# One TensorE task for both token halves of a head pair's sums, with both small PSUM banks

## The chip, the cores and the metric

One core of a Trainium2 chip runs the whole program. The metric is device microseconds for one execution. Three runs of the kernel before took 1083.85, 1081.62 and 1084.06 us, median 1083.85. The execution that was profiled took 1081.87 us by its own time, and its profile spans 1080.1 us.

## What is computed

Attention with a memory term, then two feed-forward layers, all float32:

```python
scores = scale * np.matmul(q, k.transpose(0, 1, 3, 2))     # B=4, H=8, S=576, D=64
scores = np.where(causal, -1000000000.0, scores)
a = softmax(scores)                                        # rows, + 1e-09
local = np.matmul(a, v)
mem_out = einsum(phi(q), M_prev) / (einsum(phi(q), z_prev) + 1e-06)
x = g * mem_out + (1 - g) * local                          # g = sigmoid(beta), to [2304, 512]
h = x @ w_in;  x = (h * tanh(log1p(exp(h)))) @ w_out       # d_ff = 2048
h = x @ w2_in; out = (h * cos(h)) @ w2_out
```

## The kernel before, in words

**Tasks and their order.** Every step of the work is a task with an engine, a cost, the tasks that it needs, a rank, the buffers that it takes and those that it uses (`add`, L163). `arrange` (L176) runs a model of the engines by these costs and lays the tasks out in one list; each engine then executes its own in that order, and the semaphores that the framework sets keep the data right. An engine waits at the instruction it has come to and passes none. Where TensorE (PE) would have nothing to do early in the program, `arrange` puts short dummy matmuls in (`warm`, L303).

**Attention.** Sixteen pairs of heads are done one after the other, overlapping (`pair`, L346; the pair's number stands in the tiles' names, so `pv9_0` is pair 9's). PE transposes k and q (`ptk`, `ptq`, L400), evacuated by ScalarE (ACT) or VectorE (DVE) to `kT` and `qT`, and at the last keys also to `kd`. Scores are made in three groups of rows (`s`, L491), and one small piece of 64 keys goes into a bank of its own (`sx`, L511); DVE takes the row maxima (L520, L524), ACT the exponentials (L536), DVE sums and scales (L563, L572). PE transposes the scaled rows (`t`, L587), ACT or DVE copies them to `PT`. Then the sums of heads: `pv`, L654, tokens 0 to 287 in one task (`pv..._0`, 6 matmuls), 288 to 575 in another (`pv..._1`, 10 matmuls), each evacuated to `xs` (`f_xs`) and stored to DRAM (`f_out`, L663).

**Banks.** `ptk`, `ptq`, `sx`, `t` and `pv` share two PSUM banks, the pool `misc`. A task that takes one holds it until all users of its tile are through: for `sx` that is two maxima on DVE and two exponentials on ACT. Before, each half of the sums takes one bank; `pv(1)` also names `pv(0)`'s matmuls and copy among what comes before it. `arrange` asks for each buffer that a task takes when it will be free. For the small banks it looks at the one whose turn is next; the turn moves only when the task is laid out:

```python
            o = held[b.cls][turn[b.cls] % len(held[b.cls])]      # L206, in at_free(b)
...
                    for b in t.takes:                            # L233
                        f = at_free(b)
...
                for b in t.takes:                                # L275
                    held[b.cls][turn[b.cls] % len(held[b.cls])] = b
                    turn[b.cls] += 1
```

**The rest.** From some 106 us on PE fills the time between attention's steps with the first layer's first half of d_ff, in blocks of 256 tokens (`h0`, L759, `acc0`, L802; block 0 needs the stored halves 0 of pairs 0 to 3, L699 loads it). At about 375 us attention is over. Its memory is then given to the first layer's second half and the second layer, in blocks of 384 tokens (L887, L967, L969), to the end.

Of the kernel before, what the change touches and what calls it, by code (L numbers as in the profile page):

```python
# [29 lines left out]
def tile_kernel(ctx: ExitStack, tc: tile.TileContext, q, k, v, M_prev, z_prev, beta,  # L30
                moe_w_in, moe_w_out, moe2_w_in, moe2_w_out, out):
    nc = tc.nc
    B, H, S, D = q.shape
# [129 lines left out]
    def add(eng, cost, fn, deps=(), rank=0.0, takes=(), uses=(), func=None, mode=0, lag=0.0, size=0):  # L163
        t = Task()
        t.eng, t.cost, t.fn, t.rank, t.takes = eng.split("/"), cost, fn, rank, list(takes)
        t.func, t.mode, t.lag, t.end, t.on, t.size = func, mode, lag, None, None, size
        t.deps = [d for d in deps if d is not None]
        for b in (*takes, *uses):
            b.users.append(t)
        tasks.append(t)  # L170
        return t
# [141 lines left out]
    def copy(e, dst, src, scale=None):  # L313
        if e == "act":
            nc.scalar.activation(dst, src, AF.Copy, scale=1.0 if scale is None else scale)  # L315
        elif scale is None:
            nc.vector.tensor_copy(out=dst, in_=src)  # L317
        else:
            nc.vector.tensor_scalar(out=dst, in0=src, scalar1=scale, scalar2=None, op0=ALU.mult)

    def c_act(n):
        return 0.19 + 0.00082 * n

    def c_dve(n):
        return 0.11 + 0.00106 * n

    def c_both(n):
        return (c_act(n), c_dve(n))
# [5 lines left out]
    ROWS = [D] + [P] * 4  # L334
    START = [0] + [D + P * i for i in range(4)]
    SLOTS = ((3, 0), (4,), (2, 1))
    PARTS = ((0, SH), (SH, S))
# [3 lines left out]
    def misc(name):  # L341
        return pools["misc"].tile([P, 512], F32, tag="m", name=name)
# [3 lines left out]
    def pair(m):  # L346
        b, h0 = m // NP, 2 * (m % NP)
        hp = m % NP
        d = {}
        A1, A2 = pools["a1"], pools["a2"]  # L350
        R = 100.0 * m
        B_ = {n: Buf(n) for n in ("q", "k", "v", "z", "mv", "mn", "ph", "qT", "kT", "kd", "PT", "xs")}
# [29 lines left out]
        dv = add("sp", 1.8, f_v, rank=R + 5, takes=[B_["v"], B_["mv"]], size=320)  # L382
# [206 lines left out]
        flipped = {}  # L589
# [32 lines left out]
        for x, order_ in enumerate(SLOTS):  # L622
            for i in order_:
# [6 lines left out]
                else:  # L630
                    flip(i, [(i, 0, j) for j in range(na)],
                         lambda PT, i=i, na=na: PT[:, i + 1:i + 2 + 6 * (na - 1):6, :], x)
                    flip(i, [(i, 1, i - y) for y in range(na)],
                         lambda PT, i=i, na=na: PT[:, 24 - 6 * i:24 - 6 * i + 7 * (na - 1) + 1:7, :], x)
                    if i == 4:
                        flip(4, [(4, 1, 0), (4, 0, 4)], lambda PT: PT[:, 28:30, :], x)

        def pv(x):
            lo, hi = PARTS[x]
            w = hi - lo  # L640
            bm = Buf("misc")
            s = {}
            js = [j for j in range(5) if START[j] < hi]

            def f_pv(e):
                PT, vt = d["PT"].rearrange("p b c -> p (b c)"), d["v"]
                s["o"] = o = misc(f"pv{m}_{x}")
                for j in js:
                    z_ = max(START[j], lo)
                    first_a, first_b = (7 * j + 1) * P - START[j], (24 - 6 * j) * P - START[j]  # L650
                    if j == 0:
                        first_a, first_b = first_a + D, first_b + D
                    for h, c in ((0, first_a), (1, first_b)):
                        nc.tensor.matmul(o[h * D:(h + 1) * D, z_ - lo:w], vt[:, h, j - 1, :] if j else d["mv"][:, h, :],  # L654
                                         PT[:, c + z_:c + hi], start=j == 0, stop=j == js[-1])

            def f_xs(e):
                if x == 0:
                    d["xs"] = A2.tile([P, S], F32, tag="xs", name=f"xs{m}")
                copy(e, d["xs"][:, lo:hi], s["o"][:, 0:w])  # L660

            def f_out(e):
                nc.sync.dma_start(out=x1d[b][:, hp, lo:hi], in_=d["xs"][:, lo:hi])  # L663

            need = [t_ for i in range(5) if START[i] < hi and START[i] + ROWS[i] > lo for t_ in flipped[i]]
            cost = sum(hi - max(START[j], lo) for j in js) * 4 / 2400 + 0.1
            t_p = add("pe", cost, f_pv, need + [dv, p_0], R + 60, [bm], [B_["PT"], B_["v"], B_["mv"]], mode=2)
            t_x = add("act/dve", c_both(w), f_xs, [t_p, x_0], R + 60, [B_["xs"]] if x == 0 else [], [bm] + ([B_["xs"]] if x else []))
            x1_done[m, x] = add("sp", 0.4, f_out, [t_x], -1.0, [], [B_["xs"]], size=144)
            return t_p, t_x  # L670

        p_0 = x_0 = None
        p_0, x_0 = pv(0)
        pv(1)

# [380 lines left out]
    for m in range(NJ):  # L1058
        pair(m)
# [32 lines left out]
    for i in range(4 * NFH, 8 * NFH):  # L1092
        x = i - 4 * NFH
# [36 lines left out]
```

## Time and profile before

| | |
|---|---|
| median of three runs | 1083.85 us |
| the profiled execution | 1081.87 us, span 1080.1 us |
| PE busy | 1053.2 us, 98% of the span |
| DVE, ACT busy | 761.6 us, 570.1 us |
| attention with its overlap | 0 to about 375 us |

The profile has a row for every instruction. PE's matmuls are pipelined, so the time from one row's start to the next row's start is what a group costs. Idle time before an instruction is named after the semaphore that ended it. A line of a wait names a helper (L315, L317: copies by ACT and DVE), so the tile's name says what was waited for.

### The profile page before, as it was taken

To read this page: it belongs to the slowest core of one execution; us is meant where nothing else is said; L and a number is where in the kernel's file an instruction comes from. 1 tells how busy PE (TensorE), PEld (TensorE's weight loads), DVE (VectorE), ACT (ScalarE), POOL (GpSimd) and SP (SyncE) were. 2 spreads that over 40 slices of the span, in tenths; PEclk is the share of its full clock that TensorE was granted. 3 is DMA by queue.
4 is the path that set the end of the run, shared out by engine and by line. 5 is a ranking of instruction groups with operands and counts; after the bars stand their busy time and mean duration, and the time that the engine had idled before them with its cause. 6 is when DMAs were issued, how large, how long until landed. Compare 5 with 4: busy or idle time off the path is not lost.

```text
span 1080.1 us, 17930 instructions
## 1 busy us (share of the span) xinstructions
PE 1053.2 (98%) x6938; PEld 938.7 (87%) x6938; DVE 761.6 (71%) x1694; ACT 570.1 (53%) x1279; POOL 3.8 (0%) x19
## 2 busy tenths in 40 slices
PE   8898999999999999999999999999999999999998
PEld 5666778788877899989999999998999999999997
DVE  6999997886787568757552228887666676766664
ACT  4676675676676443433323234766555555555544
POOL 1000000000000000000000000000000000000000
PEclk9999999999999999999999999999999999999999
DMA  6455423222322165446352216211000010000000
GB/s 165 114 132 161 113 55 103 69 70 67 100 69 59 44 204 156 137 135 205 102 183 88 89 59 187 79 38 59 1 30 30 1 59 2 30 30 1 30 1 30
DMA packets 112853, 88.73 MB, mean 82 GB/s; under 512 B 65792, under 2 KB 103680, under 8 KB 112768
## 3 DMA queue, kind: packets, MB, share of 16 engines
q1 hardware_dynamic: 112768, 87.58, 27.1%
q8 instruction: 55, 0.90, 0.3%
q14 instruction: 30, 0.25, 0.1%
HBM read 68.69 MB, written 18.87 MB: 81 GB/s over the span
## 4 chain that ended last, share of the span: by engine, by line
PE 88%; DVE 7%; ACT 3%; issue 1%; POOL 0%; ACTq 0%; POOLq 0%; DVEq 0%
PE h L887 28%; PE acc L969 18%; PE acc L967 9%; PE h L759 9%; PE acc L802 9%; PE pv L654 5%; PE t L587 4%; PE s L491 3%; DVE nm L520 2%; DVE p L572 1%; PE warm L303 1%; ACT p L536 1%; PE ptq L400 1%; ACT PT L315 1%; PE ptk L400 1%
## 5 line engine op out<-in xcount | busy, mean ns | idle before, releaser
L887 PE MATMUL h<-x,w 128*128 128x384 f32 x1728 | 345.0, 337 | 1.6 <-ACT g L903 1.6
L887 PEld LDWEIGHTS h<-x,w 128*128 128x128 f32 x1728 | 307.4, 188 | 17.2 <-ACT g L903 1.8
L969 PE MATMUL acc<-w,G 128*128 128x512 f32 x864 | 228.4, 393 | 0.0
L969 PEld LDWEIGHTS acc<-w,G 128*128 128x128 f32 x864 | 160.0, 188 | 22.1
L954 DVE TENSOR_TENSOR G<-g,G 128x384 fp32r<-128x384 f32 x144 | 79.8, 555 | 100.2 <-ACT G L315 99.6
L759 PE MATMUL h<-x,w 128*128 128x256 f32 x864 | 127.7, 288 | 4.6 <-DVE g L317 4.2
L802 PE MATMUL acc<-G,w 128*128 128x256 f32 x864 | 129.7, 289 | 1.1 <-ACT o L315 0.7
L759 PEld LDWEIGHTS h<-x,w 128*128 128x128 f32 x864 | 111.4, 191 | 9.0 <-DVE g L317 5.2
L315 ACT ACTIVATE G<-g 128x384 fp32r<-128x384 f32 (+1 forms) x152 | 81.2, 535 | 66.6 <-DVE g L938 35.8
L802 PEld LDWEIGHTS acc<-G,w 128*128 128x128 f32 x864 | 111.9, 191 | 4.0 <-ACT o L315 1.4
L967 PE MATMUL acc<-G,w 128*128 128x384 f32 x576 | 112.6, 336 | 0.0
L536 ACT ACTIVATE p<-s,nm 128x64 f32<-128x64 f32 (+4 forms) x160 | 81.3, 515 | 40.0 <-DVE nm L520 26.2
L967 PEld LDWEIGHTS acc<-G,w 128*128 128x128 f32 x576 | 100.9, 188 | 0.0
L931 ACT ACTIVATE n<-n 128x384 f32<-128x384 f32 x96 | 49.9, 521 | 63.5 <-DVE n L927 63.5
L903 ACT ACTIVATE g<-h 128x384 f32<-128x384 f32 x48 | 23.4, 491 | 113.1 <-PE h L887 112.2
L587 PE MATMUL t<-ident,p 128*128 128x128 f32 (+1 forms) x480 | 73.7, 277 | 7.8 <-ACT PT L315 3.7
L520 DVE TENSOR_REDUCE nm<-s 128x2 f32<-128x1024 f32 (+4 forms) x80 | 62.2, 790 | 23.5 <-PE s L495 16.4
L915 DVE TENSOR_SCALAR u<-hs 128x384 f32<-128x384 f32 x96 | 34.5, 359 | 54.6 <-ACT hs L315 51.9
L938 DVE TENSOR_TENSOR g<-n,hs 128x384 f32<-128x384 f32 x96 | 53.2, 555 | 26.3 <-ACT n L934 26.2
L587 PEld LDWEIGHTS t<-ident,p 128*128 128x128 f32 (+1 forms) x480 | 52.3, 140 | 18.5 <-ACT PT L315 7.8
L315 ACT ACTIVATE hs<-h 128x384 f32<-128x384 f32 x96 | 47.0, 490 | 39.3 <-PE h L887 36.6
L315 ACT ACTIVATE PT<-t 128x256 f32<-128x256 f32 (+3 forms) x97 | 43.4, 466 | 42.0 <-PE t L587 41.5
(91 smaller groups left out, 1243.6 us busy)
## 6 DMA issues: line engine op xcount, KB each, us to landing
raw<-in_moe_w_in_dram SPq DMA_DIRECT2D x32, 512.0 KB, 4.3
raw<-in_moe_w_out_dram SPq DMA_DIRECT2D x32, 512.0 KB, 3.8
k<-in_k_dram SPq DMA_DIRECT2D x32, 144.0 KB, 2.8
x1d<-xs SPq DMA_DIRECT2D x32, 144.0 KB, 2.1
xad<-o SPq DMA_DIRECT2D x9, 512.0 KB, 3.7
x2d<-o SPq DMA_DIRECT2D x6, 768.0 KB, 3.6
x<-x2d SPq DMA_DIRECT2D x6, 768.0 KB, 4.2
out_dram<-o SPq DMA_DIRECT2D x18, 256.0 KB, 2.0
```

Source lines behind the costliest of these rows:

```text
L315: nc.scalar.activation(dst, src, AF.Copy, scale=1.0 if scale is None else scale)
L520: nc.vector.tensor_reduce(out=s["nm"][:, c], in_=s["sp"][i], axis=AX.X, op=ALU.max, negate=True)
L536: nc.scalar.activation(d["p", i][:, j, D + lo:D + hi], src, AF.Exp, bias=s["nm"][:, c, j:j + 1], scale=1.0, accum_out=s["sm"][:, 1 if part ...
L587: nc.tensor.transpose(ps[:, at:at + r], d["p", i][0:r, h, j * P:(j + 1) * P], ident[0:r, 0:r])
L654: nc.tensor.matmul(o[h * D:(h + 1) * D, z_ - lo:w], vt[:, h, j - 1, :] if j else d["mv"][:, h, :], PT[:, c + z_:c + hi], start=j == 0, sto ...
L759: nc.tensor.matmul(h[:, half // 2], w[:, a, 0, c * P:(c + 1) * P], x[:, e_, c, :], start=c == 0 and pi == 0, stop=c == NKC - 1 and pi == 2)
L802: nc.tensor.matmul(t[:, c], w[:, a, 1, n * P:(n + 1) * P], G[:, e_, half], start=f == 0 and pi == 0 and c == 0, stop=f == NFH - 1 and pi == 2,
L887: nc.tensor.matmul(q_["h"], w[:, a, 0, c * P:(c + 1) * P], x[:, e_, c, :], start=c == 0 and pi == 0, stop=c == NKC - 1 and pi == 2)
L938: nc.vector.tensor_tensor(out=q_["g"], in0=q_["n"], in1=q_["hs"], op=ALU.mult)
L954: ENG[e].tensor_tensor(out=q_["G"][:, 1], in0=q_["g"], in1=q_["G"][:, 0].bitcast(F32), op=ALU.subtract)
L967: nc.tensor.matmul(o, w[:, a, 1, c * P:(c + 1) * P], G[:, e_, :], start=st, stop=sp_)
L969: nc.tensor.matmul(o, G[:, a, c * P:(c + 1) * P], w[:, e_, 1, :], start=st, stop=sp_)
```

## The change

The two tasks `pv(0)` and `pv(1)` become one, `f_pv`. It needs all of the pair's flipped rows, takes two buffers of the class `misc`, and issues the 6 matmuls of half 0 and then the 10 of half 1. Copies and stores stay one per half, in `out_`; both copies now need the whole task.

```diff
-        def pv(x):
-            lo, hi = PARTS[x]
-            w = hi - lo
-            bm = Buf("misc")
...
+        banks = [Buf("misc") for _ in PARTS]
+        o_ = {}
+
+        def f_pv(e):
+            PT, vt = d["PT"].rearrange("p b c -> p (b c)"), d["v"]
+            for x, (lo, hi) in enumerate(PARTS):
+                o_[x] = o = misc(f"pv{m}_{x}")
+                js = [j for j in range(5) if START[j] < hi]
                 for j in js:
...
+        cost = sum(hi - max(START[j], lo) for lo, hi in PARTS for j in range(5) if START[j] < hi) * 4 / 2400 + 0.1
+        t_p = add("pe", cost, f_pv, [t_ for l in flipped.values() for t_ in l] + [dv], R + 60, banks, [B_["PT"], B_["v"], B_["mv"]], mode=2)
+
+        def out_(x, t_x):
...
-            need = [t_ for i in range(5) if START[i] < hi and START[i] + ROWS[i] > lo for t_ in flipped[i]]
-            t_p = add("pe", cost, f_pv, need + [dv, p_0], R + 60, [bm], [B_["PT"], B_["v"], B_["mv"]], mode=2)
-            t_x = add("act/dve", c_both(w), f_xs, [t_p, x_0], R + 60, [B_["xs"]] if x == 0 else [], [bm] + ([B_["xs"]] if x else []))
+            t_x = add("act/dve", c_both(hi - lo), f_xs, [t_p, t_x], R + 60, [B_["xs"]] if x == 0 else [], [banks[x]] + ([B_["xs"]] if x else []))
             x1_done[m, x] = add("sp", 0.4, f_out, [t_x], -1.0, [], [B_["xs"]], size=144)
...
+        out_(1, out_(0, None))
```

The rest of attention is laid out anew around it, so nearly every pair's order differs. The number of warm matmuls goes from 218 to 216. All other instructions stay in number; a few copies change between DVE and ACT.

**Banks in the program as built.** In 13 of the 16 pairs the two halves lie in different banks. In pairs 1, 9 and 12 `sx` is the task that took a small bank last, its readers come later in the program, and both halves lie in one bank: there the first matmul of `pv..._1` waits for the copy of `pv..._0`. In the other pairs it waits for the copy out of whatever held the second bank. In pairs 5, 8, 13 and 15 that is one of the pair's own flipped rows, in pairs 2, 3, 4, 6, 7 and 10 a `ptk`, in pairs 0, 11 and 14 a `ptq`.

**PE at pair 9's sums**, before (`acc0` and `h0` are the first layer's; the rows left out are `s10_2` and more of these):

```order
L512 MATMUL sx10_3187<-mask2_122,ident_b_120 128x128
L802 MATMUL acc0_1_1_3007<-G0_1_3_2818,w0_6_1853 128x256 x6
L759 MATMUL h0_2_2_3016<-x2_2598,w0_5_1578 128x256 x6
L654 MATMUL pv9_0_3207<-PT9_2993,mv9_2564 64x288 x2
L654 MATMUL pv9_0_3207<-PT9_2993,v9_2561 64x224 x2
L654 MATMUL pv9_0_3207<-PT9_2993,v9_2561 64x96 x2
L802 MATMUL acc0_1_1_3007<-G0_1_3_2818,w0_7_2005 128x256 x6
L491 MATMUL s10_2_3232<-kT10_2821,qT10_2898 128x320 x2
...
L802 MATMUL acc0_2_0_3251<-G0_2_0_3106,w0_1_693 128x256 x6
L654 MATMUL pv9_1_3284<-PT9_2993,mv9_2564 64x288 x2
```

and with the change, where rows that wait for a semaphore name it:

```order
L512 MATMUL sx10_3180<-mask2_122,ident_b_120 128x128
L652 MATMUL pv9_0_3185<-PT9_2999,mv9_2535 64x288 [waits Activation_49]
L652 MATMUL pv9_0_3185<-PT9_2999,mv9_2535 64x288
L652 MATMUL pv9_0_3185<-PT9_2999,v9_2532 64x224 x2
L652 MATMUL pv9_0_3185<-PT9_2999,v9_2532 64x96 x2
L652 MATMUL pv9_1_3192<-PT9_2999,mv9_2535 64x288 [waits Activation_49]
L652 MATMUL pv9_1_3192<-PT9_2999,mv9_2535 64x288
L652 MATMUL pv9_1_3192<-PT9_2999,v9_2532 64x288 x4
```

Half 1 stood 25 rows behind half 0 and had no wait; now it stands right behind it, and waits for ACT's copy `xs9` of half 0. On ACT that copy stands here, five instructions behind the one for which half 0 waits (the first row):

```order
L315 ACTIVATE PT9_2999<-t9_1_3163 128x2x128
L315 ACTIVATE o1_2914<-acc0_1_1_2921 128x512
L431 ACTIVATE mn11_3173<-mn11_3173 128x640
L536 ACTIVATE p10_1_3178,sm10_1_3179<-s10_1_3111,nm10_1_3153 128x512 x2
L536 ACTIVATE p10_1_3178,sm10_1_3179<-sx10_3180,nm10_1_3153 128x64
L315 ACTIVATE xs9_3242<-pv9_0_3185 128x288
```

Before, that copy was one of DVE's, and no matmul of half 1 carried a wait.

**ACT at pair 4's sums**, with the change. Half 0 waits for the first row; half 1 waits for the last but one, the copies out of `ptk6_1`, which holds the second bank:

```order
L315 ACTIVATE PT4_1452<-t4_1_1566 128x2x128
L140 ACTIVATE w0_4_1450<-dec0_4_1_1513 128x512
L315 ACTIVATE kT6_1502<-ptk6_1_1569 128x288
L315 ACTIVATE x1_1454<-x1_1454 128x512 x2
L431 ACTIVATE mn5_1603<-mn5_1603 128x640
L140 ACTIVATE w0_5_1616<-dec0_5_0_1554 128x512
L315 ACTIVATE kd0_130<-ptk6_1_1569 64x64 x2
L315 ACTIVATE xs4_1634<-pv4_0_1585 128x288
```

Before, `ptk6_1` came after pair 4's sums, and half 1 waited for `ptq5_1` on PE itself and nothing on ACT. PE's rows between `t4_1_1566` and half 0 are now `ptk6_1` and one `h0` group of six.

**DVE at pair 1's sums**, before:

```order
L563 SCALAR_TENSOR_TENSOR sm2_0_802<-sm2_0_802,ginv_137 128x4
L564 RECIPROCAL sm2_0_802<-sm2_0_802 128x4
L317 COPY xs1_860<-pv1_0_833 128x288
L572 TENSOR_SCALAR p2_0_801<-p2_0_801,sm2_0_802 128x448 x2
L572 TENSOR_SCALAR p2_0_801<-p2_0_801,sm2_0_802 128x64 x2
```

and with the change:

```order
L520 TENSOR_REDUCE nm2_1_857<-s2_1_811 128x2
L142 TENSOR_TENSOR w0_1_649<-dec0_1_1_571,w0_1_649 128x512
L563 SCALAR_TENSOR_TENSOR sm2_0_824<-sm2_0_824,ginv_137 128x4
L564 RECIPROCAL sm2_0_824<-sm2_0_824 128x4
L524 TENSOR_REDUCE nm2_1_857<-sx2_831 128x2
L526 TENSOR_TENSOR nm2_1_857<-nm2_1_857 128x2
L572 TENSOR_SCALAR p2_0_823<-p2_0_823,sm2_0_824 128x448
L317 COPY xs1_887<-pv1_0_838 128x288
```

The copy for which half 1 waits has three more instructions between it and the reciprocal, and `sm2_0` needs three exponentials that ACT has behind its copy of pair 1's last flipped rows. Pair 12's copy `xs12` stands likewise on DVE: behind `sm13_0`, its reciprocal and two scalings of 448 columns, all after ACT's four exponentials of `s13_0`.

## Rows read from the trace of the kernel before

**Rows 1.** The page of the kernel before, its first two lines: span, engines' busy time.

```profile
span 1080.1 us, 17930 instructions
...
PE 1053.2 (98%) x6938; PEld 938.7 (87%) x6938; DVE 761.6 (71%) x1694; ACT 570.1 (53%) x1279; POOL 3.8 (0%) x19
```

**Rows 2.** Busy time by stretch: us; PE, PEld, DVE, ACT, POOL (instructions); clock; DMA share; GB/s.

```profile
40.00:106.00 66.00, 58.68 (x490) 41.08 (x489) 62.88 (x169) 44.77 (x142) 0.00 (x0) 1.00 0.53 138
106.00:160.00 54.00, 50.30 (x429) 40.14 (x429) 51.83 (x121) 36.85 (x97) 0.00 (x0) 1.00 0.33 89
...
200.00:376.00 176.00, 173.81 (x1482) 143.88 (x1481) 131.98 (x343) 111.66 (x296) 0.00 (x0) 1.00 0.24 65
```

**Rows 3.** Waits of PE over the span: who for whom, total us, times, longest us.

```profile
PE warm L303 <- DVE zeros L300: 2.0, 1, 2.0
PE pv L654 <- DVE PT L317: 1.8, 2, 1.3
...
PE pv L654 <- DVE xs L317: 0.2, 1, 0.2
```

**Rows 4.** Waits of PE from 106 to 376 us.

```profile
PE h L759 <- DVE g L317: 3.5, 6, 1.0
```

**Rows 5.** Timeline around pair 7's sums: start us, us, engine, line, operation, tiles, shapes, count.

```profile
179.74 0.71 PE L654 MATMUL pv<-PT,mv 128*64 128x288 f32 x4
...
180.92 0.44 PE L400 MATMUL ptq<-ident,q 128*128 128x128 f32 x2
...
182.00 0.71 PE L654 MATMUL pv<-PT,mv 128*64 128x288 f32 x4
...
184.25 1.02 PE L491 MATMUL s<-kT,qT 64*128 64x448 f32 x4
```

**Rows 6.** Timeline around pair 1's first sum, PE, DVE and ACT.

```profile
52.98 0.71 PE L654 MATMUL pv<-PT,mv 128*64 128x288 f32 x4 [0.55 <-DVE PT L317]
53.04 0.28 DVE L524 TENSOR_REDUCE nm<-sx 128x2 f32<-128x128 f32 x1
...
53.61 0.69 ACT L536 ACTIVATE p<-s,nm 128x512 f32<-128x512 f32 x1 [0.49 <-DVE nm L526]
54.04 0.16 DVE L563 SCALAR_TENSOR_TENSOR sm<-sm,ginv 128x4 f32<-128x4 f32 x1
...
54.29 0.68 ACT L536 ACTIVATE p<-s,nm 128x512 f32<-128x512 f32 x1
54.32 0.43 DVE L317 COPY xs<-pv 128x288 f32<-128x288 f32 x1
...
54.66 1.13 DVE L572 TENSOR_SCALAR p<-p,sm 128x448 f32<-128x448 f32 x4
...
54.95 0.31 ACT L536 ACTIVATE p<-sx,nm 128x64 f32<-128x64 f32 x1
```

**Rows 7.** ACT groups to 376 us, shapes apart: busy us, mean ns | idle before.

```profile
L536 ACT ACTIVATE p<-s,nm 128x448 f32<-128x448 f32 x32 | 20.2, 631 | 8.3 <-DVE nm L520 8.2
...
L431 ACT ACTIVATE mn<-mn 128x640 f32<-128x640 f32 x16 | 11.8, 740 | 0.2
...
L315 ACT ACTIVATE kT<-ptk 128x288 f32<-128x288 f32 x26 | 10.6, 409 | 13.5 <-PE ptk L400 13.3
L140 ACT ACTIVATE w<-dec 128x512 fp32r<-128x512 f32 x16 | 10.0, 626 | 4.2 <-DVE dec L131 4.1
...
L315 ACT ACTIVATE x<-x 128x512 fp32r<-128x512 f32 x12 | 6.9, 625 | 0.0
...
L315 ACT ACTIVATE kd<-ptk 64x64 f32<-64x64 f32 x24 | 5.1, 213 | 0.5 <-DVE kT L317 0.4
```

**Rows 8.** PE group of the warm matmuls, same columns.

```profile
L303 PE MATMUL warm<-zeros,ident_b 128*128 128x256 bf16 x218 | 31.1, 285 | 2.0 <-DVE zeros L300 2.0
```

**Rows 9.** Timeline of SP: pair 3's second store, block 0's load.

```profile
95.09 0.54 SPq L663 DMA_DIRECT2D x1d<-xs  x1
...
96.16 0.56 SPq L699 DMA_DIRECT2D x<-x1d  x1
```

More of the change, by code (lines that the diff above doesn't have):

```diff
@@ L636, in pair @@
                         flip(4, [(4, 1, 0), (4, 0, 4)], lambda PT: PT[:, 28:30, :], x)
-        def pv(x):
-            lo, hi = PARTS[x]
-            w = hi - lo
-            bm = Buf("misc")
[L642 to L647, printed above, removed]
+        banks = [Buf("misc") for _ in PARTS]
[5 more added lines that the diff above has]
+                js = [j for j in range(5) if START[j] < hi]
                 for j in js:
@@ L653, in f_pv @@
                     for h, c in ((0, first_a), (1, first_b)):
-                        nc.tensor.matmul(o[h * D:(h + 1) * D, z_ - lo:w], vt[:, h, j - 1, :] if j else d["mv"][:, h, :],
+                        nc.tensor.matmul(o[h * D:(h + 1) * D, z_ - lo:hi - lo], vt[:, h, j - 1, :] if j else d["mv"][:, h, :],
                                          PT[:, c + z_:c + hi], start=j == 0, stop=j == js[-1])
+        cost = sum(hi - max(START[j], lo) for lo, hi in PARTS for j in range(5) if START[j] < hi) * 4 / 2400 + 0.1
+        t_p = add("pe", cost, f_pv, [t_ for l in flipped.values() for t_ in l] + [dv], R + 60, banks, [B_["PT"], B_["v"], B_["mv"]], mode=2)
+        def out_(x, t_x):
+            lo, hi = PARTS[x]
             def f_xs(e):
@@ L659, in f_xs @@
                     d["xs"] = A2.tile([P, S], F32, tag="xs", name=f"xs{m}")
-                copy(e, d["xs"][:, lo:hi], s["o"][:, 0:w])
+                copy(e, d["xs"][:, lo:hi], o_[x][:, 0:hi - lo])
             def f_out(e):
                 nc.sync.dma_start(out=x1d[b][:, hp, lo:hi], in_=d["xs"][:, lo:hi])
-            need = [t_ for i in range(5) if START[i] < hi and START[i] + ROWS[i] > lo for t_ in flipped[i]]
-            cost = sum(hi - max(START[j], lo) for j in js) * 4 / 2400 + 0.1
-            t_p = add("pe", cost, f_pv, need + [dv, p_0], R + 60, [bm], [B_["PT"], B_["v"], B_["mv"]], mode=2)
-            t_x = add("act/dve", c_both(w), f_xs, [t_p, x_0], R + 60, [B_["xs"]] if x == 0 else [], [bm] + ([B_["xs"]] if x else []))
+            t_x = add("act/dve", c_both(hi - lo), f_xs, [t_p, t_x], R + 60, [B_["xs"]] if x == 0 else [], [banks[x]] + ([B_["xs"]] if x else []))
             x1_done[m, x] = add("sp", 0.4, f_out, [t_x], -1.0, [], [B_["xs"]], size=144)
[L670 to L674, printed above, removed]
+            return t_x
+        out_(1, out_(0, None))
     TBS = (T0, T1, T1)
```

## The prediction, made before the changed kernel ran

> **What bounds the kernel now.** I read the busy line first: PE is busy for 1053.2 of 1080.1 us [rows 1]. The kernel is as long as PE's work plus the time in which PE waits or runs warm matmuls, so a change of order can only pay by shortening those. The windows say where they are [rows 2]. From 40 to 160 us (two windows, 120 us) DVE is busy for 62.88 + 51.83 = 114.7 us, 96%, and PE leaves 7.3 + 3.7 = 11.0 us idle: PE is paced by DVE there. From 200 to 376 us PE is busy for 173.81 of 176 us while DVE is at 75% and ACT at 63%. Every microsecond that PE stands still there is a microsecond of the kernel. Next, the waits of PE: the sums lose 1.8 us to their own flipped rows, in two waits, and 0.2 us to copies of a first half [rows 3]. So little is to be won at the place of the change. The timeline gives the two pieces: half 0 costs 180.92 - 179.74 = 1.18 us, half 1 costs 184.25 - 182.00 = 2.25 us, and what stands between them, there and in all 16 pairs, is work that has to be done anyway [rows 5].
>
> **What the change does, part by part.**
>
> *Removed.* The gap before half 1: 0.2 us by name, and some shorter ones that have no name; I take 0.5 us. It can't be over 0.2 + 1.8 = 2.0 us, if the waits for flipped rows go too [rows 3]. Two warm matmuls of 218: 31.1 us / 218 = 0.14 us each [rows 8], 0.3 us.
>
> *Added: a wait in the middle of the sums.* The planner asks twice for the bank whose turn it is, so the second bank is never asked about. On the chip the first matmul of half 1 waits for what holds that bank, with all of PE's later work queued behind it. Half 0 covers 1.18 us of that wait. Where the holder is the pair's own flipped rows (4 pairs), or a transposed k or q whose copies stand right behind the flipped rows' copy, that is enough: one kT copy of 0.41 us and two kd copies of 0.21 us are 0.8 us [rows 7]. I cost those at nothing; without half 0 as cover they would cost that 0.8 us a pair. Four pairs are different.
>
> Pair 9: one bank for both halves, so half 1 waits for ACT's copy of half 0. In ACT's queue before it: o and mn, two exponentials of 512 at 0.68 us (53.61 to 54.29 in the row) and one of 64 at 0.31. Low end, by the same chain at pair 1: from the sum's start at 52.98 to the end of the first sx exponential at 54.95 + 0.31, and the copy 0.43, is 2.7 us; less 1.18 us of half 0 makes 1.5 us [rows 6]. High end: o at 0.63 us (as the 512-wide x copies) and mn at 0.74 come on top [rows 7], 2.9 us. PE has an accumulation group and sx to do before half 0, which hides about half of those two: 2.2 us.
>
> Pair 12: the same bank again, the copy is DVE's. After the flipped rows' copy ACT does four exponentials, 2 x 0.63 [rows 7] + 2 x 0.31 = 1.9 us; then DVE needs 0.28 us for the sums and their reciprocal, two scalings of 1.13 / 4 = 0.28 and the copy, 0.43 [rows 6], together 3.15 us; less 1.18 is 2.0 us. PE comes late to half 0 by an accumulation group, as much as 0.9 us: low end 1.1. If DVE is still in its maxima when the exponentials want them, about 1 us later: 3.0. I take 2.2 us.
>
> Pair 1: the same bank, DVE again. Low end: the row's copy began 0.16 us after half 0 was through (54.32 against 52.98 + 1.18); put the maximum of sx (0.28, its combination about 0.15) and one scaling (0.28) in front, and with the copy it is 1.3 us [rows 6]. High end: if the three exponentials start only when half 0 is released (0.63 + 0.31 + 0.31) and the work ahead on DVE runs late, 2.7 us. I take 2.0 us.
>
> Pair 4: two banks, but the second is held by k of pair 6, and ACT does w, kT, two x copies, mn, w and two kd first: 0.63 + 0.41 + 1.25 + 0.74 + 0.63 + 0.43 = 4.1 us [rows 7]. ACT gets a lead of some 1 us, a transpose and six matmuls on PE; 4.1 - 1.0 - 1.18 = 1.9 us. Ends: 1.0 with a lead of 2 us, 2.9 with none.
>
> *What of it is paid.* Pairs 9 and 12 stand where PE is the bound: 4.4 us, all of it. Pairs 1 and 4 stand where DVE paces PE. DVE keeps working while PE stalls, and later waits of PE there (3.5 us for copies of h alone [rows 4]) shrink by what DVE has caught up; but DVE then wants the next scores, which PE delivers late by the whole stall. Neither end is excluded, 0 or 3.9 us; I take half, 2.0 us.
>
> *Moved.* Copies and stores: half 0's store now leaves with half 1's. Who waits for it is block 0's load, and on SP's queue that load stood behind the second store already (95.09, then 96.16) [rows 9]. No cost; a copy earlier by half 1's 2.25 us would have been of no use. Single copies that go from DVE to ACT: 0.41 us for the 288-wide kT copy [rows 7], on an engine with room: nothing. The rest of attention in another order: no term, since its work is the same; its share of the uncertainty is bounded by PE's idle time there.
>
> **Sum.** 4.4 + 2.0 - 0.5 - 0.3 = +5.6 us on the profiled execution's 1081.87 us: 1087.5. The median of the runs, 1083.85, lies 2.0 us above that execution, so I forecast **1089.4 us** as a median. About 0.3% (3.3 us) is what a measurement of this kernel can tell from no change: below 1080.6 is faster, above 1087.1 slower.
>
> **The rivals.**
>
> *Absorbed.* Pairs 1 and 4 cost nothing and pairs 9 and 12 their low ends: 1.5 + 1.1 - 0.8 = +1.8 us, 1085.7. For it: PE's 11 us of idle time under a DVE at 96% [rows 2]. Against it: warm matmuls are fixed in the program and don't shrink to make room. Chance 0.27.
>
> *Faster.* The two halves back to back in two banks, with copies that are through in time: PE loses 2.0 us of waits at the sums and the warm 0.3, and where DVE gets 2.25 us more per pair without a new h to copy, most of the 3.5 us of [rows 4]; less 1.5 us of rests of the four stalls, about -4 us: 1079.9. It decides at the four copies: each would have to end within about half a microsecond after half 0. The rows speak against it, since what stands ahead of each is over 2 us by itself. By the Trainium skill, page "Perfetto Trace Analysis", section "Optimizing Tensor Performance", independent groups of matmuls should rotate through different banks, so that one's evacuation lies beside the next one's matmuls. By that rule taken alone the change gains the 2.0 us of waits and the time is this rival's. The trace of before can't bear it out, as its gap is 0.2 us. Chance 0.10.
>
> *More.* All four stalls are paid at their high ends, 2.9 + 3.0 + 2.7 + 2.9 - 0.3 = +11.2 us, 1095.0. It holds if ACT and DVE run late against PE in general. A worse form: the granted clock falls. It is 1.00, that is 2.4 GHz, in the stretches of [rows 2]; but PE's longest wait anywhere is 2.0 us, at the very start [rows 3], and stalls of 2 to 3 us would be longer than any. At 1.2 GHz half 1 after each stall would take 4.5 us for 2.25, +9 us for four. The Trainium skill's page "TensorE: Matmul & The Clock Gate", Part 1, says that an array that has been idle is throttled to half. Chance of both forms 0.13, of the second 0.03.
>
> **How the numbers follow.** The forecast has 0.50, between +3.3 and +9 us. Slower is forecast and "more": 0.63; the same is "absorbed": 0.27; faster 0.10. The range leaves out the faster case and the far part of "more". It begins at pairs 9 and 12 with their low ends, 2.6 us, less the most that can be saved, 2.3: +0.3 us, 1084.1, and ends at +11.2 us, 1095.0.
>
> **What will show it.** In the waits of PE a line for pv with a copy of xs, on DVE twice and ACT once, 1 to 3 us each, and one for pv with kd: together 5 to 11 us where 0.2 us stood. Half 1's first matmul starts 3 us or more after half 0's in pairs 1, 4, 9 and 12, and 1.2 us after in the other twelve. From 200 us to the end of attention PE's idle time goes from 2.2 us to 6 or 7. Idle time from 40 to 160 us says how much of pairs 1 and 4 is paid: 13 us if half, 11 if none. The granted clock stays 1.00. The forecast is wrong if these waits are there and the time is not (absorption), if they are under 1 us (the queues were ahead), or if some other wait of PE changes by more than 2 us.

## The result and the profile after

The change is slower. Its runs took 1096.13, 1096.13, 1099.05 and 1099.13 us, median 1097.59, against 1083.84 us for the kernel before beside them. The medians lie 13.75 us apart; the ratio of the runs is 1.0139, 95% interval 1.0126 to 1.0152, which is some 15 us. Below, a ratio of another run is turned into us on 1082 us, the kernel before beside the later runs, so 0.0010 is 1.1 us; the intervals are about 1.5 us to either side. The prediction, 1089.4 us with a range to 1095.0, had the direction and was too small.

First the page of the changed kernel (its profiled execution took 1096.13 us), to be held against [rows 1].

```profile
span 1094.4 us, 17936 instructions
...
PE 1055.7 (96%) x6936; PEld 938.7 (86%) x6936; DVE 757.6 (69%) x1687; ACT 574.5 (52%) x1286; POOL 3.8 (0%) x19
```

The span is 14.3 us longer. PE is busy 2.5 us longer, though two warm matmuls went, and idle for 1094.4 - 1055.7 = 38.7 us, where it was 1080.1 - 1053.2 = 26.9: 11.8 us more. DVE and ACT together do the same work as before. The windows of [rows 2] show where PE stands:

```profile
40.00:106.00 66.00, 57.84 (x485) 39.64 (x484) 60.26 (x161) 41.98 (x137) 0.00 (x0) 1.00 0.49 132
106.00:160.00 54.00, 46.31 (x369) 36.15 (x365) 47.37 (x115) 34.27 (x94) 0.00 (x0) 0.97 0.32 89
200.00:376.00 176.00, 167.86 (x1434) 137.05 (x1435) 135.18 (x355) 113.70 (x308) 0.00 (x0) 0.99 0.25 65
```

Idle in the first two windows: 8.2 + 7.7 = 15.9 us, where 11.0 stood. In the third: 8.1 us, where 2.2 stood. And the granted clock, the third number from the end, is no longer 1.00 in two of them. DVE is busy for 107.6 of 120 us in the first two windows, 90% and no longer 96%: it stands still more often as well.

The waits of PE over the span, the rows of pv of over 1 us (as [rows 3]) and two others:

```profile
PE pv L652 <- DVE xs L317: 4.4, 2, 2.3
...
PE pv L652 <- ACT xs L315: 2.2, 1, 2.2
...
PE ptq L400 <- ACT PT L315: 1.9, 3, 0.7
PE h L758 <- DVE g L317: 1.8, 3, 0.8
PE pv L652 <- ACT kd L315: 1.6, 1, 1.6
```

The four foretold waits are there: 4.4 + 2.2 + 1.6 = 8.2 us (by the timeline 2.15 in pair 1, 1.64 in pair 4, 2.18 in pair 9, 2.28 in pair 12); in the other twelve pairs half 1 follows half 0 at once, but for 0.23 us in pair 10. The two waits of pv for flipped rows, 1.8 us, are down to 0.2. So the sums account for some 6.4 of the 11.8 us, and other waits for the remaining 5.4.

The timeline of PE at pair 9's sums, in the window from 238 to 246 us, and the clock there and behind pair 4:

```profile
241.63 1.23 PE L652 MATMUL pv<-PT,mv 128*64 128x288 f32 x4 [2.18 <-ACT xs L315]
242.65 2.83 PE L652 MATMUL pv<-PT,v 128*64 128x288 f32 x16
245.41 0.81 PE L491 MATMUL s<-kT,qT 64*128 64x320 f32 x4
```

```profile
241.00:245.00 4.00, 3.37 (x16) 1.80 (x18) 1.35 (x5) 0.88 (x5) 0.00 (x0) 0.57 0.07 16
149.00:153.00 4.00, 3.96 (x22) 3.16 (x24) 2.85 (x12) 2.04 (x8) 0.00 (x0) 0.57 0.32 73
```

Half 1 takes 245.41 - 241.63 = 3.78 us, where it takes 2.25 at full clock [rows 5]: right behind the wait the clock fell to the lower level, 1.2 GHz, for most of it. These two stretches are the only falls in this execution, and the 2.5 us by which PE is busy longer are put down to them. By the Trainium skill, page "TensorE: Matmul & The Clock Gate", Part 1, an idle array is throttled to half. The row agrees in that; the wait before this fall was 2.18 us. But behind the longest of the four waits, in pair 12, half 1 ran at full clock:

```profile
307.11 0.71 PE L652 MATMUL pv<-PT,mv 128*64 128x288 f32 x4 [2.28 <-DVE xs L317]
307.64 1.79 PE L652 MATMUL pv<-PT,v 128*64 128x288 f32 x16
```

So it did in pairs 1 and 4. One of the four waits was followed by a fall, and the fall at 149 us came behind waits for the decoded weights (0.5 and 1.0 us).

What the prediction got wrong shows best at pair 1. Timeline from 52 to 62 us, PE and then DVE of the kernel before, then PE and DVE of the change:

```profile
54.16 0.81 PE L491 MATMUL s<-kT,qT 64*128 64x320 f32 x4
...
55.72 0.71 PE L654 MATMUL pv<-PT,mv 128*64 128x288 f32 x4
```

```profile
55.71 0.29 DVE L549 TENSOR_TENSOR p<-ph,den 128x128 f32<-128x128 f32 x1
55.91 0.82 DVE L520 TENSOR_REDUCE nm<-s 128x2 f32<-128x640 f32 x1
```

```profile
52.13 0.71 PE L652 MATMUL pv<-PT,mv 128*64 128x288 f32 x4 [0.20 <-ACT PT L315]
...
55.53 0.71 PE L652 MATMUL pv<-PT,mv 128*64 128x288 f32 x4 [2.15 <-DVE xs L317]
56.07 1.79 PE L652 MATMUL pv<-PT,v 128*64 128x288 f32 x16
57.79 0.81 PE L491 MATMUL s<-kT,qT 64*128 64x320 f32 x4
```

```profile
56.08 0.28 DVE L549 TENSOR_TENSOR p<-ph,den 128x128 f32<-128x128 f32 x1
59.24 0.82 DVE L520 TENSOR_REDUCE nm<-s 128x2 f32<-128x640 f32 x1 [2.88 <-PE s L495]
```

Before, the next scores stood between the halves, 54.16 us, and DVE went from its scalings to their maxima without a pause. Now they stand behind half 1 and its wait, 57.79 us, and DVE stands still for 2.88 us. DVE does work on while PE waits, until 56.36 us; but it isn't ahead for that. It runs out of scores, which come later by the wait and by the whole of half 1: 57.79 - 52.13 = 5.7 us behind the start of half 0, where it was 54.16 - 52.98 = 1.2.

### The profile page after: what moved, and what is told of

Read it like the earlier page. It is cut to its first block, busy times and chain, and to the rows that moved or that the text cites. A ratio compares the mean times of both kernels' runs of the same rounds, so it can differ in the third digit from the quotient of the medians.

```text
span 1094.4 us, 17936 instructions
## 1 busy us (share of the span) xinstructions
PE 1055.7 (96%) x6936; PEld 938.7 (86%) x6936; DVE 757.6 (69%) x1687; ACT 574.5 (52%) x1286; POOL 3.8 (0%) x19
## 4 chain that ended last, share of the span: by engine, by line
PE 87%; DVE 10%; ACT 2%; issue 1%; POOL 0%; ACTq 0%; POOLq 0%
PE h L886 28%; PE acc L968 18%; PE acc L966 9%; PE h L758 9%; PE acc L801 9%; PE pv L652 4%; PE t L587 4%; PE s L491 4%; DVE nm L520 2%; DVE p L572 2%; DVE PT L317 1%; PE warm L303 1%; PE ptq L400 1%; ACT p L536 1%; DVE dec L128 1%
## 5 line engine op out<-in xcount | busy, mean ns | idle before, releaser
L315 ACT ACTIVATE G<-g 128x384 fp32r<-128x384 f32 (+1 forms) x158 | 84.9, 538 | 70.1 <-DVE g L937 35.5
L536 ACT ACTIVATE p<-s,nm 128x320 f32<-128x320 f32 (+4 forms) x160 | 81.3, 516 | 36.5 <-DVE nm L520 25.9
L315 ACT ACTIVATE PT<-t 128x512 f32<-128x512 f32 (+3 forms) x91 | 42.6, 482 | 49.4 <-PE t L587 48.7
```

The source lines that it names most:

```text
L536: nc.scalar.activation(d["p", i][:, j, D + lo:D + hi], src, AF.Exp, bias=s["nm"][:, c, j:j + 1], scale=1.0, accum_out=s["sm"][:, 1 if part ...
```

## The experiments

The theories, with the letters that the expectations use. **H**: the hidden bank waits, each paid in full, and the clock behind them are the whole loss (H+: with a spread of the orders on top). **A**: the waits of pairs 1 and 4 are absorbed, as the prediction half assumed. **O**: the joined order costs by itself, whatever the four waits do. **O'** and **L**: every new order of this planner is a draw with a spread of many us. **J**: joined sums make worse orders even where the planner knows both banks. The table has each run's ratio to the kernel before beside it, and of its profiled execution PE's idle time (span less busy) and mean granted clock.

| run | ratio (95% interval) | PE idle us | clock |
|---|---|---|---|
| the kernel before | 1 | 26.9 | 1.000 |
| the change | 1.0139 (1.0126 to 1.0152) | 38.7 | 0.997 |
| e2_copies_early | 1.0047 (1.0031 to 1.0064) | 32.0 | 0.998 |
| e2_pairs_9_12 | 1.0107 (1.0092 to 1.0122) | 35.2 | 0.995 |
| e2_pairs_1_4 | 1.0096 (1.0080 to 1.0111) | 35.5 | 0.997 |
| e3_before_two_pairs | 1.0040 (1.0025 to 1.0054) | 30.1 | 0.998 |
| e5_before_pair_1 | 1.0037 (1.0024 to 1.0050) | 29.4 | 0.997 |
| e6_before_twelve_pairs | 1.0055 (1.0038 to 1.0071) | 34.3 | 0.998 |
| e4_before_all_pairs | 1.0151 (1.0133 to 1.0168) | 42.2 | 0.993 |
| e1_two_banks_asked | 1.0002 (0.9992 to 1.0011) | 28.0 | 1.000 |
| j1_joined_asked_order_b | 1.0003 (0.9994 to 1.0012) | 25.5 | 1.000 |
| j2_joined_asked_order_c | 1.0034 (1.0022 to 1.0047) | 30.0 | 0.998 |
| p2_asked_planned_again | 1.0128 (1.0113 to 1.0143) | 36.6 | 0.994 |
| e7_banks_kept_free | 1.0097 (1.0080 to 1.0113) | 33.5 | 0.997 |
| s1_split_order_b | 1.0008 (0.9998 to 1.0017) | 27.4 | 0.998 |
| s2_split_order_c | 1.0006 (0.9997 to 1.0016) | 26.8 | 1.000 |
| p1_before_planned_again | 1.0025 (1.0016 to 1.0034) | 28.2 | 0.998 |
| p3_change_planned_again | 1.0119 (1.0104 to 1.0134) | 37.3 | 0.996 |
| b2_joined_order_c | 1.0162 (1.0141 to 1.0184) | 40.3 | 0.994 |
| b1_joined_order_b | 1.0182 (1.0167 to 1.0197) | 40.9 | 0.992 |

**The four waits mended, TensorE's order kept.** The list of tasks is planned as in the change; only then are the copies moved forward in it:

```diff
+    ahead = {}
+
     def run(order):
+        for x, after in ahead.values():
+            order.remove(x)
+            order.insert(order.index(after) + 1, x)
...
+                if m == 6:
+                    ahead["kd"] = (got[key, x][1], ev)
...
+            first = t_x is None
             t_x = add("act/dve", c_both(hi - lo), f_xs, [t_p, t_x], ...
+            if first and m in (1, 9, 12):
+                ahead[m] = (t_x, t_p)
```

> The changed kernel with TensorE's order as it is; only the copies for which half 1 of a sum waits are written earlier: the xs copy of half 0 right behind the sum in pairs 1, 9 and 12, and the decay copies of one k transpose (pair 4's wait) right behind that transpose's own copy. Theory H (the hidden bank wait and what it drags along is the whole loss): the four waits shrink from 8.2 us to some 2, the clock does not fall to 1.2 GHz, the decode waits behind pair 4 go; 1086 to 1089 us. Theory O (the replanned order costs by itself, whatever the four waits do): only the 6.2 us of the waits come back at most, 1091 to 1094 us. Theory A (pairs 1 and 4 lie where DVE is the bound and cost nothing; pairs 9 and 12 pay): about 1092 us.

Measured 1.0047: 10.0 us of 15 are back, 5.1 remain. The four waits fell from 8.2 to 1.6 us (now all for copies of a half), and from 200 to 376 us the clock is full:

```profile
PE pv L659 <- DVE xs L322: 1.1, 2, 0.6
...
PE pv L659 <- ACT xs L320: 0.5, 1, 0.5
```

```profile
200.00:376.00 176.00, 169.81 (x1456) 140.07 (x1455) 133.28 (x350) 115.51 (x305) 0.00 (x0) 1.00 0.28 78
```

The time, 1087.85 us, lies where H had it. In the profiled executions PE's idle time shrank by 38.7 - 32.0 = 6.7 us for 6.6 us of wait, and its busy time by 1.2 us with one fall of the clock less. But H as the whole loss would leave nothing, and idle time is still 5.1 us over the kernel before, 4.0 of them from 200 to 376 us (6.2 us idle in the row above, 2.2 in [rows 2]). And one of H's signs failed: the clock is down from 146 to 150 us, as it was at 149, with pair 4's wait gone.

**Two pairs at a time.** The same edit with `m in (9, 12)` and without the decay copies, and with `m == 1` and the decay copies.

> The changed kernel with the xs copy of half 0 written earlier in pairs 9 and 12 alone (the stretch where TensorE is the bound); pairs 1 and 4 keep their waits of 2.2 and 1.6 us. Theory H: the waits of 4.4 us shrink to about 1 and the fall of the clock in pair 9 (about 1.5 us) goes, 1091 to 1093 us; the clock's fall at 149 us stays. Theory A: these two pairs held all that is paid, so the time comes to where the run with all four pairs mended stands, within 1 us. Theory O: 1094 us.

> The changed kernel with the copies of pairs 1 and 4 alone written earlier; pairs 9 and 12 keep their waits of 2.2 and 2.3 us. With all four mended 9.7 us came back against the change (1.0139 to 1.0047), with pairs 9 and 12 mended 3.4 us. Theory H (each wait is paid in full, wherever it lies): the 3.8 us of these two waits come back and the falls of the clock that followed them, so 5 to 7 us less than the change, ratio 1.008 to 1.0095. Theory A (the waits of pairs 1 and 4 are absorbed where DVE sets the pace): under 2 us less, ratio 1.012 or more.

Measured: 3.5 us back for pairs 9 and 12, whose waits shrank by 3.4 us, and 4.7 us back for pairs 1 and 4, whose waits shrank by 3.2. Each difference is uncertain by some 2 us, but PE's idle time says the same: 38.7 - 35.2 = 3.5 and 38.7 - 35.5 = 3.2 us less. Theory A falls: the two waits in the stretch where DVE is the busiest engine are paid in full. With pairs 1 and 4 mended pair 9 still waits and half 1 is slow; with pair 9 mended it isn't. Timelines at pair 9, first of the run with pairs 1 and 4 mended, then with 9 and 12:

```profile
236.37 0.71 PE L659 MATMUL pv<-PT,mv 128*64 128x288 f32 x4 [2.19 <-ACT xs L320]
236.90 3.31 PE L659 MATMUL pv<-PT,v 128*64 128x288 f32 x16
```

```profile
242.94 0.71 PE L659 MATMUL pv<-PT,mv 128*64 128x288 f32 x4 [0.51 <-ACT xs L320]
243.47 1.79 PE L659 MATMUL pv<-PT,v 128*64 128x288 f32 x16
```

The time with pairs 9 and 12 mended, 1094.23 us, is nonetheless over H's 1093 and where O had it: its profiled execution has three falls of the clock before 160 us, where the change's had one. The first is behind pair 1's wait, which is as long as in the change, where no fall came:

```profile
55.37 0.71 PE L659 MATMUL pv<-PT,mv 128*64 128x288 f32 x4 [2.15 <-DVE xs L322]
55.91 2.62 PE L659 MATMUL pv<-PT,v 128*64 128x288 f32 x16
```

**Joining without planning anew.** In the kernel before half 1's matmuls are moved right behind half 0's in the list, in chosen pairs, with the same `run` as above and nothing else:

```diff
-        pv(1)
+        p_1 = pv(1)[0]
+        if m in (9, 12):
+            ahead[m] = (p_1, p_0)
```

> The kernel before, nothing planned anew: only in pairs 9 and 12 half 1 of the sum is moved right behind half 0, where both have the same bank, so half 1 waits for the xs copy of half 0. Theory H: each wait costs its length and what the clock does after it, 2 x 2.2 us and up to 1.5 us a wait for the clock: 1088 to 1091 us. Theory O (order, not waits): within 1 us of the kernel before, 1084 to 1085 us, since the order of the rest is the same and the work that stood between the halves only comes later.

> The kernel before, nothing planned anew: in pair 1 alone (53 us into the span, DVE the busiest engine there) half 1 is moved right behind half 0 in the same bank and waits for the xs copy, about 2 us. Theory H: 2 us longer, ratio 1.0015 to 1.0025, more if the clock falls behind it. Theory A: absorbed, ratio 1.000 to 1.0008.

> The kernel before, nothing planned anew: in the twelve pairs whose halves lie in different banks half 1 is moved right behind half 0; pairs 1, 6, 9 and 12, where a shared bank would make half 1 wait for the xs copy, stay as they are. Theory H (only waits for the xs copy cost): ratio 0.999 to 1.001. Theory O (joining the halves by itself takes work away that hid copies, some 3 us as in the changed kernel with its four waits mended): ratio 1.002 to 1.004.

> The kernel before, nothing planned anew: in all 16 pairs half 1 is moved right behind half 0; in pairs 1, 6, 9 and 12 it waits for the xs copy. By theory H the sum of the parts: about 4 us of the two waits in pairs 9 and 12 (measured 1.0040 with them alone), 2 each for pairs 1 and 6, and nothing for the twelve: ratio 1.006 to 1.009. By theory A pairs 1 and 6 add nothing: 1.004. By theory O the twelve pairs add 3 us: 1.009 to 1.012, with the clock's falls on top.

Measured +4.3, +4.0, +6.0 and +16.3 us; the third is over O's 1.004 (by its interval it reaches it), and the last over every range that was written down, though O put falls of the clock on top. H was near the size of the first and wrong in its reason: the waits for xs were not 2.2 us but about 0.6 each; two other waits of 1.1 us come with them, of transposes (t) for copies of xs and kT, and the clock falls once. Pair 1 alone shows what costs. Its timeline from 52 to 63 us, PE, then DVE and ACT, and the clock behind it:

```profile
55.35 0.71 PE L659 MATMUL pv<-PT,mv 128*64 128x288 f32 x4 [0.58 <-DVE xs L322]
55.89 1.79 PE L659 MATMUL pv<-PT,v 128*64 128x288 f32 x16
57.61 0.81 PE L496 MATMUL s<-kT,qT 64*128 64x320 f32 x4
62.60 1.11 PE L592 MATMUL t<-ident,p 128*128 128x128 f32 x4 [2.79 <-ACT xs L320]
```

```profile
59.06 0.82 DVE L525 TENSOR_REDUCE nm<-s 128x2 f32<-128x640 f32 x1 [2.51 <-PE s L500]
62.14 0.41 ACT L320 ACTIVATE xs<-pv 128x288 f32<-128x288 f32 x1
```

```profile
61.00:69.00 8.00, 6.08 (x32) 4.49 (x33) 5.95 (x18) 3.71 (x11) 0.00 (x0) 0.57 0.28 86
```

The wait between the halves is only 0.58 us. But the scores come 57.61 - 54.16 = 3.4 us later than before (0.55 us of that lay ahead of the pair already), DVE waits 2.51 us for them, and ACT's exponentials come later with DVE's maxima (59.98 for 56.83 us). Behind these exponentials in ACT's queue stands the copy of half 1, whose bank PE's next transposes need. PE waits for it 2.79 us, where the kernel before had

```profile
59.44 0.66 PE L587 MATMUL t<-ident,p 128*128 128x128 f32 x4 [0.83 <-ACT xs L315]
```

So the lateness comes back to PE as a wait, and behind that wait the clock is down. Of the 5.4 us by which this span is longer, 2.5 us are idle time of PE (29.4 less 26.9): the 0.58 and the 2.79 - 0.83 = 1.96. The other 2.9 us are busy time, 1056.1 less 1053.2. The twelve pairs, none of which shares a bank between its halves, cost 6.0 us all the same, against H, in waits of PE that the kernel before doesn't have, or has at 0.2 us (pv for qT):

```profile
PE sx L516 <- DVE xs L322: 2.4, 3, 1.6
...
PE t L592 <- ACT qT L320: 1.2, 1, 1.2
PE pv L659 <- DVE qT L324: 1.1, 1, 1.1
PE ptq L405 <- ACT w L140: 1.1, 1, 1.1
```

Three of these are banks: sx finds its bank held until a sum's copy, and t and pv find one held by a transposed q. So in an order made for separate halves, what stood between them covered copies, and without it PE meets them unfinished. All 16 pairs joined this way cost as much as the change; the three parts with pair 6, which no run has by itself, make up the sum: 4.3 + 4.0 + 6.0 = 14.3 of 16.3 us.

**Both banks asked for.** The planner looks at the first and at the second bank of a task, not twice at the first:

```diff
-        def at_free(b):
+        def at_free(b, ahead=0):
...
-            o = held[b.cls][turn[b.cls] % len(held[b.cls])]
+            o = held[b.cls][(turn[b.cls] + ahead) % len(held[b.cls])]
...
-                    for b in t.takes:
-                        f = at_free(b)
+                    for z, b in enumerate(t.takes):
+                        f = at_free(b, sum(y.cls == "misc" for y in t.takes[:z]) if b.cls == "misc" else 0)
```

> The changed kernel with the planner asking for each of the two small banks apart, so that a sum starts only when the second bank is free too; the whole order is planned anew by that. Theory H: no wait between halves in any pair, 1084 to 1089 us. Theory O: a sum that must find both banks free starts late, the P transposes and other users of the banks are moved, and the idle time turns up ahead of the sums instead: 1091 us or more, with the waits of 8.2 us gone and others of that size in their place.

Measured 1.0002: all 15 us are back, with the halves joined in every pair. H seemed proved, O to fall. Since any such edit gives a whole new order, the orders themselves had to be drawn more than once, by 0.1 us (or 0.05) more or less in the planner's cost of the sum, which computes the same:

```diff
-        cost = sum(hi - max(START[j], lo) for lo, hi in PARTS for j in range(5) if START[j] < hi) * 4 / 2400 + 0.1
+        cost = sum(hi - max(START[j], lo) for lo, hi in PARTS for j in range(5) if START[j] < hi) * 4 / 2400 + 0.2
```

> The kernel before with 0.1 us added to the planner's cost of each half's sum, which changes nothing that is computed but gives another order from the first pair on. It measures what another order alone is worth. Theory H: an order whose bank waits the planner knows stays within 0.3% of the kernel before, ratio 0.998 to 1.003. Theory O' (any new order costs or gives several us by chance, so that the change's loss says little about the joining): outside 0.997 to 1.004.

> The changed kernel with 0.1 us added to the planner's cost of the joined sum: another order, in which two pairs (2 and 11) have both halves in one bank and wait for the xs copy, instead of three such pairs and pair 4's wait in the change. Theory H (hidden waits, each paid in full, plus the falls of the clock behind them): two waits of about 2 us and up to 2 us of clock each, ratio 1.003 to 1.008, so better than the change's 1.0139. Theory O' : no relation to the number of waits, anything from 1.000 to 1.015.

> The changed kernel with both small banks asked for by the planner, and 0.1 us added to its cost of the joined sum: another order without a hidden wait. Theory H: as the first such order, ratio 0.998 to 1.003, and the clock full in nearly all executions. Theory O': outside that.

> The changed kernel with both small banks asked for, and a rule added: while a joined sum that is due lacks its second bank, no task of a later rank takes a small bank. An attempt at a version that is faster than both: the sum no longer starts late, so the copies behind it come earlier. Theory H gives 1080 to 1083 us, at most 2 us under the kernel before, since nothing in the trace showed a gap between the halves that was idle; if keeping a bank empty starves the transposes and score sums that use it, 1084 to 1090 us with waits of TensorE for them.

Measured 1.0025, 1.0119, 1.0128 and 1.0097. H had 1.003 to 1.008 for the second and at most 1.003 for the third; the fourth is over both ends of what was expected. The change's other order (1.0119) has two pairs with a shared bank and is hardly better than the change, and the joined sum with both banks asked for now costs 13.9 us though its longest wait between halves is 0.4 us. H in its pure form falls, and O' has both. In that run PE waits about as long as in the change, elsewhere:

```profile
PE t L587 <- DVE PT L317: 5.2, 9, 2.2
PE h L758 <- ACT g L315: 4.2, 4, 2.1
PE acc L801 <- ACT G L315: 2.7, 2, 2.4
...
PE h L758 <- ACT x L315: 1.9, 1, 1.9
```

```profile
196.00:199.00 3.00, 0.75 (x6) 0.47 (x5) 2.93 (x9) 1.44 (x3) 0.00 (x0) 1.00 0.94 298
199.00:206.00 7.00, 4.95 (x22) 4.46 (x21) 6.69 (x14) 6.02 (x10) 0.00 (x0) 0.52 0.19 41
```

Four waits of about 2 us again, and here the clock is down behind all of them: behind two in the row above, and from 264 to 268 and from 400 to 404 us. The rule that keeps banks free (a task of a later rank takes no small bank while a due sum lacks one) was meant to beat both kernels and didn't:

```diff
+                kept = min((r[0] for r in ready[e] if r[3].on is None and len(r[3].takes) == 2 and r[2] <= now), default=1e9)
                 for r in ready[e]:
...
+                    if rank > kept and any(b.cls == "misc" for b in t.takes):
+                        continue
```

Then more orders of each of the three kinds:

> The kernel before (halves apart) with the planner's cost of each half's sum 0.1 us less: another order. Theory J (joined sums make worse orders): 1.000 to 1.004, as the kernel before (1) and its first other order (1.0025). Theory L (an order is a draw; the two joined orders of 1.013 and the one of 1.000 are of the same lot as the orders with halves apart): now and then 1.008 or more here too.

> The kernel before (halves apart) with 0.05 us more in the planner's cost of each half's sum: another order. Theory J: 1.000 to 1.004. Theory L: spread like the joined ones, 1.000 to 1.013.

> The joined sum with both banks asked for and 0.1 us less in the planner's cost of it: another order without a hidden wait for an xs copy. Theory J: 1.006 to 1.014, the first such order (1.0002) was the lucky one. Theory L: anything from 1.000 to 1.013, as the orders with halves apart. Theory H (only hidden waits cost): 1.000 to 1.003, already contradicted by 1.0128 of the other such order.

> The joined sum with both banks asked for and 0.05 us more in the planner's cost of it: another order. Theory J: 1.006 to 1.014. Theory L: anything from 1.000 to 1.013. Theory H: 1.000 to 1.003.

> The changed kernel (joined, the second bank not asked for) with 0.1 us less in the planner's cost of the joined sum: another order, with both halves in one bank in five pairs (1, 6, 9, 12, 14) and a wait for decay copies in two (2, 4). Theory H+ (each hidden wait is paid in full with up to 2 us of clock behind it, and an order has a spread of some 3 us, at times 13, on top): seven waits, ratio 1.013 to 1.022. Theory L (the order is a draw whatever the hidden waits): 1.000 to 1.013.

> The changed kernel (joined, the second bank not asked for) with 0.05 us more in the planner's cost of the joined sum: another order, with both halves in one bank in three pairs (10, 12, 13). Theory H+: three waits of about 2 us and the clock, ratio 1.006 to 1.014. Theory L: anything from 1.000 to 1.013, as likely under 1.004 as the orders without a hidden wait are (three of four).

Measured, in order: 1.0008, 1.0006, 1.0003, 1.0034, 1.0182, 1.0162. J falls by the third and fourth. H+ has the fifth, and no theory had the sixth. L, one spread for all, doesn't fit the first kind below, where no order is over 1.0025. By kind: halves apart 1, 1.0006, 1.0008, 1.0025; joined with both banks asked for 1.0002, 1.0003, 1.0034, 1.0128 (and 1.0097 under the added rule); joined with the second bank not asked for 1.0119, 1.0139, 1.0162, 1.0182. The third kind lies apart from the first in every draw, so the change's loss is not a chance of one order. In it the ratio rises with the number of pairs whose halves share a bank: 1.0119 with two, 1.0139 and 1.0162 with three, 1.0182 with five, some 2.3 us a pair. Drawn on to none, these four points would leave some 8 us. That is an estimate from few points, as the waits in such pairs run from 0.5 to 2.9 us; it goes with the 5.1 us left when the waits of the change were mended. The waits at the sums are only part of what such an order costs. In the run at 1.0162 the waits of pv include

```profile
PE pv L652 <- ACT xs L315: 7.2, 3, 2.8
...
PE pv L652 <- ACT p L536: 2.0, 1, 2.0
```

The waits for xs are 7.2 us of the 13.4 by which its idle time stands over the kernel before. The second kind can be as good as the kernel before, but not better in any of its draws, and one of them was nearly as bad as the change; why that one went wrong is open beyond its waits. With that draw, asking for both banks is not shown to be the cure. Nor does it rule out a long wait between halves: in the order at 1.0034 one half waits 1.95 us for a copy of kT.

## Why the prediction was wrong, point by point

- **What bounds it**: right that PE's idle time counts, but its work is of fixed length only at a full clock. 14.3 us of span are 11.8 us of idle PE and 2.5 us of PE at the low clock.
- **The four waits**: right, in their places, releasers and sizes. Foretold 2.2, 2.2, 2.0 and 1.9 us, measured 2.18, 2.28, 2.15 and 1.64. That each came within 0.3 us is in part luck, since each was picked from ends 1.4 to 1.9 us apart. In pair 1 DVE was late by its own maxima and weights, without a pause, and not by waiting for exponentials. Right too that the other twelve pairs cost nothing here (0.23 us in pair 10).
- **"Removed"**: too small. 0.5 us was taken; the waits for flipped rows and for the half went from 2.0 to 0.2 us, near the most that was named.
- **Pairs 9 and 12, paid in full**: right. Mending 3.4 us of wait gave 3.5 us back. Idle time from 200 to 376 us came to 8.1 us where 6 or 7 was foretold, so 1.5 us of other waits came on top.
- **Pairs 1 and 4, paid by half**: this step failed. "DVE keeps working while PE stalls" was so, but nothing was saved by it. "PE delivers late by the whole stall" was the end to take, and short of the mark: the next scores stand behind half 1 as well, so they came later by the stall and by half 1, and DVE stood still 2.88 us. Mending 3.2 us of wait took 3.2 us of idle time away, and idle time from 40 to 160 us came to 15.9 us, where 13 stood for half and 11 for none. The rows to see this were there: [rows 6] has DVE's work up to the scalings, and the scores that feed it next lie between the two halves on PE, as `s10_2` does in the list of PE's rows at pair 9.
- **"Moved: no term"**: this step failed too. What stood between the halves had to be done anyway, but by when it was done mattered. With the four waits all but gone 5.1 us remain, and joining the twelve pairs that share no bank costs 6.0 us in the old order. It isn't a price of joining as such: three of the four orders in which the planner knew both banks (without the added rule) stand within 0.34% of the kernel before. Which moved piece of work costs what in the change stays open. "If some other wait of PE changes by more than 2 us" was named as a sign of being wrong, and one did: h for g fell from 4.2 to 1.8 us, as others rose.
- **The clock at 1.00**: failed; a fall had a chance of 0.03. The size that was named, 9 us for four falls, was too much: PE's 2.5 us are two falls in this execution, and only one of them is behind one of the four waits.
- **The rivals**: "more" came, by a sum that its text had not: sizes as forecast, all of them paid, and the clock and the order on top. "Absorbed" fell with theory A. "Faster" didn't come even where no half waits over some 0.5 us: 1.0002 and 1.0003. By the Trainium skill, page "Perfetto Trace Analysis", section "Optimizing Tensor Performance", independent groups should rotate through the banks; here both halves do, and nothing is gained, as PE had other work in the gap.

Put together for the profiled execution: +6.4 us of waits at the sums, +5.4 us of other waits, +2.5 us of clock, 14.3 in all. The 5.4 us are the sum of many small rows and are not taken apart further.

## What to carry to other kernels

DVE, 96% busy, gave no slack to PE, which feeds it: before a stall is called absorbed, look for the next instruction that it waits for, and whether that stands behind the stall in the feeder's queue. When two tasks are joined, cost what stood between them as work that comes later by the whole second task. The bank that the planner didn't ask for cost 1.2 to 1.8% in all four orders drawn without it. One good order is no proof of an edit (1.0002, then 1.0128 by the same edit): draw several of each kind.

## What the runs showed of the hardware

In mid-kernel TensorE's clock fell to 1.2 GHz behind some waits of about 2 us and not behind others: 0.57 granted from 241 to 245 us, after 2.18 us of waiting in pair 9, but 1.00 after 2.15 us in pair 1 and 2.28 us in pair 12. The same 2.15 us in pair 1 were followed by a fall in the run with pairs 9 and 12 mended, and so were 2.79 us in the run with pair 1 joined, and all four waits of 1.9 to 2.4 us in the run at 1.0128. At 149 us it fell behind waits of 0.5 and 1.0 us, and in the kernel before waits of 1.1 us (s for p) and 1.0 us (h for g) between 106 and 160 us left it at 1.00 [rows 2], so the length of one wait doesn't settle it; what does is open. Executions of one kernel differ in it: the change took 1096.13 us at a mean clock of 0.997 and 1099.1 at 0.994; the kernel before, beside the run e2_copies_early, 1081.3 to 1082.2 us at 1.000 and 1083.8 to 1084.1 at 0.998; its variant with pairs 9 and 12 joined 1085.1 to 1085.7 at 1.000 and 1088.1 at 0.998. That is 2 to 3 us between executions of the same program. It may be why the profiled execution of the kernel before, at full clock, lay 2 us under its median.
